# A spectral filter and an MLP on one core: the inverse column transform folded over f and -f, and sums moved between engines

## The chip, the core and the metric

The kernel runs on one core of a Trainium2 chip. A core has five engines that run at the same time, each with its own list of instructions: TensorE (PE in the profile; its weight loads are PEld) for matmuls and transposes, VectorE (DVE), ScalarE (ACT), GpSimd (POOL) and SyncE (SP), which here issues every DMA. Matmuls write into PSUM, eight banks of 128 partitions by 512 fp32 columns; all else lies in SBUF. An engine works through its list in order, and waits on semaphores for others. The metric is the device time of one execution in microseconds; lower is better. The median before is 391.79 us (three runs, 391.14 to 392.72).

## The reference

```python
mod = (_silu(c) @ w_mod).reshape(1, 6, 1, 512)
sa, ca, ga, sb, cb, gb = mod
h = layernorm(x) * (1 + ca) + sa                 # x: 2048 x 512
x = x + ga * irfft2(rfft2(h) * (w_r + 1j * w_i))
h = layernorm(x) * (1 + cb) + sb
x = x + gb * (mish(h @ w1 + b1) @ w2)            # w1: 512 x 1376, w2: 1376 x 512
```

Six vectors of 512, made from a conditioning vector c, shift, scale and gate two branches. The first branch is a filter in the frequency plane: a real two-dimensional FFT, a product with a complex weight, the inverse. The second is a dense layer, Mish, and a dense layer.

## The kernel before

There are no FFT instructions: the transforms are matmuls with constant matrices. The 2048 rows are split as 128 x 16, the 512 columns as 128 x 4, so that a transform is one matmul over 128 points and one small matrix over 16 and 4 points, which sits on the partitions (16 x 4 complex numbers are 128 real ones). One core does everything in four stages, and SBUF holds x throughout.

1. *Rows and columns forward* (0 to 50 us). For each n of 16, `p1_row` multiplies a transposed tile of x with row constants, and `p1_col` applies the column transform over 128 points. The result is `a_sb`.
2. *The frequency plane* (50 to 99 us, lines 374 to 597). The 64 column frequencies q go in 17 groups of up to four, in the order `seq`; group 0 (the frequencies 0, 64, 128 and so on) is special. For a group, `p2_in` transposes on TensorE and ScalarE copies to SBUF (GpSimd adds the shift's share to column 0), `p2_mul` multiplies with `kf` (the small transforms), `p2_prod` takes the complex product with the weights (two products on VectorE, a difference and a sum mostly on GpSimd), `p2_back` transposes back and ScalarE copies, `p2_out` multiplies with `kv` (the small inverse transforms), and `store_d` copies into `dd` on ScalarE, in three planes: real, imaginary, and minus real. The steps of different groups overlap in an order written out by hand (`manual_schedule`): step s does the products of group s, the `kf` matmuls of group s + 1, the copies in of group s + 3, the transposes back of group s - 2 and the `kv` matmuls of group s - 3. Between them stand pieces of the six vectors: `mod_fetch` loads a tile of `w_mod`, `mod_late` adds it up on VectorE (`mod_step` for the two gates, `mod_column` for scale and shift of the second norm), `mod_gate` multiplies the first gate into the row constants `kiv` (step 7), `apply_gate` spreads the second gate over all partitions by a matmul, at the stage's end.
3. *Columns and rows back* (99 to 146 us). `p3_col(n)` undoes the column transform with eight matmuls of 128 x 128: for each of four pieces, one over the planes real and imaginary with the constants `kc[0]` and one over imaginary and minus real with `kc[1]`. ScalarE copies the bank, `p3_row(n)` does four matmuls with `kiv`, and VectorE adds the result to x and takes the statistics of the second norm (`norm_sums`). Beside this, the MLP's weights are prepared: `load_w1` and `split_w1` cut w1 into a high and a low half (ScalarE casts, GpSimd subtracts), through two buffers; `load_w2`, `sum_w2` (GpSimd) and `split_w2` (ScalarE and VectorE) prepare w2 and sums of its blocks, which live in `modr[:, 0:2]`.
4. *The MLP* (146 to 389 us). Eight blocks of 256 rows, in each six pieces of the 1376 columns: `up`, `front`, `back` (Mish and four sums on VectorE, line 779), `halves` (high and low halves), `down`, where `down` runs two pieces behind `up`; `residual` multiplies with the second gate and adds to x.

SP's queue and each engine's list are in the order of the program. Buffers of the pool `work` come in twos per tag (`t`, `y`, `g1`, `g2`, `h`), and so do the PSUM banks A to D; a write waits for the last reader of the buffer before last. The tiles of the pool `big` share space by tag (`da`, `db`, `cr`, `ci`) from stage to stage.

## Time and profile before

| | |
|---|---|
| median of three runs | 391.79 us |
| the profiled execution | 391.52 us (span 389.4 us from the first to the last instruction) |
| TensorE busy | 383.1 us (98%) |
| VectorE, ScalarE, GpSimd busy | 298.8, 247.9, 96.1 us |
| bytes moved by DMA | 36.44 MB |
| granted TensorE clock | 1.000 |

In a line of a timeline stand the start in us, the duration, the engine, the line of the kernel, the operation, what is written and read, the shape, and the count where equal instructions are merged; in square brackets the idle time before and what ended it. A duration reaches from the start to the end on the engine, so it holds time in which the instruction was held up. One fp32 matmul stands as two instructions. In a table of stages each engine's busy time is given for the stretch named at the left, then the granted clock, the DMA engines' share and the rate.

### The profile page before, as it was taken

Reading aid. Unit: us, or ns where it says so; the run is one execution under the profiler, and the core shown is the slowest. Engines: PE = TensorE matmul, PEld = TensorE weight load, DVE = VectorE, ACT = ScalarE, POOL = GpSimd, SP = SyncE. Lnnn points to the kernel's source line nnn. Section 1 sums busy time; section 2 is a strip of 40 time slices with the busy share of each in tenths; the row PEclk is TensorE's granted clock in tenths of the full one; section 3 lists DMA queues with packets and bytes.
Section 4 is the critical chain, followed back from the end, with each engine's and each line's share of the span. In section 5 each row is a group of like instructions: output and inputs, shape, how many; then the busy total and the mean of one; then the engine's idle time right before and its main releaser. Section 6 shows DMA issues by size and latency. Waiting matters only on the chain.

```text
span 389.4 us, 7386 instructions
## 1 busy us (share of the span) xinstructions
PE 383.1 (98%) x2752; PEld 355.4 (91%) x2752; DVE 298.8 (77%) x668; ACT 247.9 (64%) x546; POOL 96.1 (25%) x132
## 2 busy tenths in 40 slices
PE   8999999999999999999999999999999999999996
PEld 8889889999999998999998998999999999899984
DVE  2888978876299989887856965965966875987993
ACT  1798756678559648975855765674674674594751
POOL 0687737665077533300000000000000010017000
PEclk9999999999999999999999999999999999999999
DMA  7999993472132411100100100100100200123011
GB/s 237 383 323 339 347 344 109 133 300 63 47 124 78 145 49 28 56 3 0 56 0 3 54 2 0 56 0 2 55 2 0 76 0 2 46 65 106 3 54 54
DMA packets 21027, 36.44 MB, mean 94 GB/s; under 512 B 3680, under 2 KB 6592, under 8 KB 20736
## 3 DMA queue, kind: packets, MB, share of 16 engines
q1 hardware_dynamic: 20992, 35.98, 27.1%
q8 instruction: 21, 0.34, 0.3%
q14 instruction: 14, 0.11, 0.1%
HBM read 31.78 MB, written 4.19 MB: 92 GB/s over the span
## 4 chain that ended last, share of the span: by engine, by line
PE 86%; DMA 4%; DVE 3%; ACT 3%; issue 1%; SPq 1%; POOL 1%; POOLq 0%; DVEq 0%
PE bank L805 24%; PE bank L752 20%; PE bank L754 10%; PE bank L482 3%; PE bank L528 3%; PE bank L673 3%; PE bank L663 3%; PE bank L664 3%; PE bank L797 2%; PE bank L248 2%; DMA x<-in_A_x_dram 2%; PE bank L203 2%; PE bank L817 2%; PE bank L642 2%; PE bank L461 2%; DMA mraw<-in_km_dram 2%
## 5 line engine op out<-in xcount | busy, mean ns | idle before, releaser
L762 ACT ACTIVATE buf<-bank,b1n 128x256 f32<-128x256 f32 (+1 forms) x88 | 40.8, 472 | 66.8 <-PE bank L754 66.4
L763 DVE TENSOR_TENSOR buf<-buf,bank 128x256 f32<-128x256 f32 (+1 forms) x88 | 35.4, 417 | 38.6 <-ACT buf L762 38.6
L715 DVE TENSOR_TENSOR al<-buf,ah 128x512 fp32r<-128x512 f32 (+2 forms) x85 | 53.5, 653 | 0.7 <-ACT ah L714 0.7
L734 POOL TENSOR_TENSOR buf<-buf,modr 128x512 f32<-128x512 f32 (+1 forms) x3 | 3.9, 1292 | 183.0 <-DMA buf<-in_B_w_dram 175.7
L752 PE MATMUL bank<-h2e,w1h 128*128 128x512 f32 (+1 forms) x176 | 48.4, 397 | 0.0
L752 PE MATMUL bank<-h2o,w1h 128*128 128x512 f32 (+1 forms) x176 | 48.3, 396 | 0.0
L714 ACT CAST ah<-buf 128x512 fp32r<-128x512 f32 (+2 forms) x85 | 43.0, 548 | 1.2 <-DVE buf L779 1.2
L779 DVE TENSOR_TENSOR buf<-buf 128x128 f32<-128x128 f32 x148 | 39.9, 311 | 3.5 <-ACT buf L769 2.2
L769 ACT ACTIVATE buf<-buf 128x512 f32<-128x512 f32 (+1 forms) x48 | 28.6, 596 | 14.8 <-DVE buf L763 14.7
L805 PE MATMUL bank<-w2a,ah 128*128 128x256 f32 x161 | 34.9, 286 | 0.0
L752 PEld LDWEIGHTS bank<-h2o,w1h 128*128 128x128 f32 (+1 forms) x176 | 30.2, 187 | 4.5
L752 PEld LDWEIGHTS bank<-h2e,w1h 128*128 128x128 f32 (+1 forms) x176 | 30.1, 187 | 4.5
L805 PE MATMUL bank<-w2b,ah 128*128 128x256 f32 x147 | 31.8, 283 | 0.0
L754 PEld LDWEIGHTS bank<-h2o,w1l 128*128 128x128 f32 (+1 forms) x176 | 26.7, 185 | 4.2
L754 PEld LDWEIGHTS bank<-h2e,w1l 128*128 128x128 f32 (+1 forms) x176 | 26.7, 185 | 4.2
L754 PE MATMUL bank<-h2e,w1l 128*128 128x256 f32 (+1 forms) x176 | 27.8, 280 | 0.0
L754 PE MATMUL bank<-h2o,w1l 128*128 128x256 f32 (+1 forms) x176 | 27.8, 280 | 0.0
L805 PEld LDWEIGHTS bank<-w2a,ah 128*128 128x128 f32 x161 | 26.7, 191 | 0.0
L663 PE MATMUL bank<-kc,d 128*128 128x128 f32 x128 | 24.7, 275 | 0.0
L664 PE MATMUL bank<-kc,d 128*128 128x128 f32 x128 | 24.7, 275 | 0.0
L805 PEld LDWEIGHTS bank<-w2b,ah 128*128 128x128 f32 x147 | 24.6, 191 | 0.0
L117 DVE BATCH_NORM_STATS2 st<-x 128x6 f32<-128x512 f32 x32 | 22.1, 689 | 0.8 <-DMA x<-in_A_x_dram 0.4
(227 smaller groups left out, 1002.7 us busy)
## 6 DMA issues: line engine op xcount, KB each, us to landing
buf<-in_B_w_dram SPq DMA_DIRECT2D x20, 256.0 KB, 2.8
x<-in_A_x_dram SPq DMA_DIRECT2D x16, 256.0 KB, 4.9
xring<-in_x_t_dram SPq DMA_DIRECT2D x16, 256.0 KB, 5.1
wm<-in_w_mod_dram SPq DMA_DIRECT2D x16, 256.0 KB, 4.2
out_dram<-x SPq DMA_DIRECT2D x7, 512.0 KB, 2.6
mraw<-in_km_dram SPq DMA_DIRECT2D x16, 128.0 KB, 5.0
wqa<-in_w_q_dram SPq DMA_DIRECT2D x8, 256.0 KB, 4.8
wqb<-in_w_q_dram SPq DMA_DIRECT2D x8, 256.0 KB, 5.5
```

Source lines behind the costliest of these rows:

```text
L117: nc.vector.bn_stats(t, x[:, n, :])
L663: nc.tensor.matmul(o, dj[:, 0:128], kc[0][:, n, :], start=True, stop=False)
L664: nc.tensor.matmul(o, dj[:, 64:192], kc[1][:, n, :], start=False, stop=True)
L714: nc.scalar.copy(h, r)
L715: nc.vector.tensor_tensor(l, r, plain(h), op=ALU.subtract)
L752: nc.tensor.matmul(ps, w1h[:, k, fs], h[:, k], start=(k == 0), stop=False)
L754: nc.tensor.matmul(ps[:, 0:256], w1l[:, k, fs], h[:, k, 0], start=False, stop=(k == 3))
L762: nc.scalar.activation(o, ps[:, 256:], AF.Identity, bias=b1n[:rows, f:f + 1])
L763: nc.vector.tensor_tensor(o, o, ps[:, 0:256], op=ALU.add)
L769: nc.scalar.activation(o, o, AF.Mish)
L779: nc.vector.tensor_tensor(o, p, q, op=op)
L805: nc.tensor.matmul(o, a[p][:, e], w2[t][q][:, r], start=(own and half == 0 and t == 1 and i == 0), stop=(end and i == 2 and (n, half) != ( ...
```

## The change

- `p3_col` has four matmuls of 128 x 128 instead of eight. For that, the frequencies f of the column transform are numbered so that partition p holds f = p for p under 64, f = -(p - 63) for 64 to 126, and 64 for partition 127 (constants and weights are laid out to match). On the way back, the sum and the difference of the values at f and -f are taken first (`fold`, VectorE: two instructions of 4 x 63 columns, one operand in SBUF and the other in the PSUM bank of the transpose). `dd` then has two planes and one set of constants `kc`; `store_d` has three copies, two of them on 63 partitions only.
- The fold of group s - 3 stands at step s, a step behind the copy, and `p2_out` moves from s - 3 to s - 4; there is a step more.
- The frequency 64 of every group is collected in `zh` by a small copy in `p2_in`, and goes through its own product and transforms (`half_mul`, `half_prod`, `half_back`, `half_out`) in steps 14 to 17; a DMA within SBUF puts it into partition 127 of `dd`.
- Group 0 is rewritten in the same manner: six copies and four folds instead of reversed copies.
- The first gate's sums run on GpSimd (`mod_step`: a scaling, and a sum for all but the first) in steps 3, 5, 7 and 9, and `mod_gate` in step 12. The second gate's sums run on GpSimd in the MLP, after its items 2 and 3, from one load of 1 MB behind the third stage; `apply_gate` runs after item 5.
- w1 goes through six buffers instead of two: two of `g2` and two each of the tags `ah` and `al`; five loads are issued at step 0 of the third stage.
- The low half of the sums of w2's tile 2 is computed on GpSimd, not VectorE. The places of some tiles in `big` change.

```diff
+H = P // 2
+U = P - 1
...
-    def mod_step(acc, w, k, eng):
-        one = sc[:, k:k + 1]
-        if k == 0:
-            eng.tensor_scalar(acc, w, one, 0.0, op0=ALU.mult, op1=ALU.add)
-        else:
-            eng.scalar_tensor_tensor(acc, w, one, acc, op0=ALU.mult, op1=ALU.add)
+    def mod_step(acc, w, k):
+        nc.gpsimd.tensor_scalar(w if k else acc, w, sc[:, k:k + 1], 0.0, op0=ALU.mult, op1=ALU.add)
+        if k:
+            nc.gpsimd.tensor_tensor(acc, acc, w, op=ALU.add)
...
-    def store_d(ps, q0, nq):
+    dd = big.tile([P, 4 * N2, 2, NQ], F32, name="dd", tag="dd")
+
+    def store_d(ps, q0, nq, end=U):
         src = ps[:, 0:nq * 128].rearrange("p (q a c) -> p a c q", q=nq, c=2)
-        for i in range(2):
-            dst = dd[i].rearrange("p n d c q -> p (n d) c q")
-            s = src[:, 32 * i:32 * i + 32]
-            nc.scalar.copy(dst[:, :, 0:2, q0:q0 + nq], s)
-            nc.scalar.mul(dst[:, :, 2, q0:q0 + nq], s[:, :, 0, :], -1.0)
+        qs = slice(q0, q0 + nq)
+        nc.scalar.copy(dd[0:H, :, :, qs], src[0:H])
+        nc.scalar.mul(dd[H:end, :, 0, qs], src[H:end, :, 1, :], -1.0)
+        nc.scalar.copy(dd[H:end, :, 1, qs], src[H:end, :, 0, :])
...
+    def fold(z, far):
+        nc.vector.tensor_tensor(z[..., H:U], z[..., 1:H], far, op=ALU.subtract)
+        nc.vector.tensor_tensor(z[..., 1:H], z[..., 1:H], far, op=ALU.add)
...
+    def half_out():
+        pd = bank("D")
+        nc.tensor.matmul(pd[:, 0:NQ], kv[:, 512:640], st.pop(("t", "h"))[:, 0:NQ], start=True, stop=True)
+        nc.scalar.copy(zh, pd[:, 0:NQ])
+        nc.sync.dma_start(dd[U:P].rearrange("p a c q -> p (a c) q")[:, :, 1:NQ], zh[:, 1:NQ])
...
-        t = buf("t")
-        nc.scalar.copy(t[:, 0:w], pc[:, 0:w])
-        st["t", g] = t
+        tv, src = (v[:, 0:w].rearrange("p (q s) -> p q s", s=P) for v in (buf("t"), pc))
+        nc.scalar.copy(tv[:, :, 0:H], src[:, :, 0:H])
+        st["t", g] = tv, src
...
-        for s in range(len(seq) + 3):
+        for s in range(len(seq) + 4):
             mod_fetch(s + 2)
+            if s >= 4:
+                p2_out(seq[s - 4])
+            if 3 <= s < len(seq) + 3:
+                p2_fold(seq[s - 3])
...
-            if s >= 3:
-                p2_out(seq[s - 3])
-            if s == 7:
+            if s == 12:
                 mod_gate()
...
+            for i, fn in enumerate((half_mul, half_prod, half_back, half_out)):
+                if s == len(seq) - 3 + i:
+                    fn()
...
-        r = buf("g2")[:, 0:hi - lo]
+        r = (buf("g2") if i % 3 == 0 else act.tile([P, 512], F32, name="wr", tag=("", "ah", "al")[i % 3]))[:, 0:hi - lo]
...
-        for j in range(4):
-            dj = d[:, j].rearrange("p c q -> p (c q)")
-            o = pe[:, j * P:(j + 1) * P]
-            nc.tensor.matmul(o, dj[:, 0:128], kc[0][:, n, :], start=True, stop=False)
-            nc.tensor.matmul(o, dj[:, 64:192], kc[1][:, n, :], start=False, stop=True)
+        for j in range(4):
+            nc.tensor.matmul(pe[:, j * P:(j + 1) * P], dd[:, 4 * n + j].rearrange("p c q -> p (c q)"), kc[:, n, :],
+                             start=True, stop=True)
...
-            split(h[:, 768:], l[:, 768:], tsum.rearrange("p e d -> p (e d)"))
+            split(h[:, 768:], l[:, 768:], tsum.rearrange("p e d -> p (e d)"), nc.gpsimd if t == 2 else nc.vector)
...
-        if s < 12:
-            load_w1(s)
+        for i in range(0 if s == 0 else s + 4, min(s + 5, 12)):
+            load_w1(i)
...
+    load_gate()
     split_w2(0, False)
...
         if s in (2, 3):
             split_w2(4, s == 3)
+            for k in (2 * s - 4, 2 * s - 3):
+                mod_step(modr[:, 2], late["g"][:, k], k)
+        if s == 5:
+            apply_gate()
```

160 lines of the change are left out of this document (99 added, 61 removed).

## The prediction, made before the changed kernel had run

> **What bounds the kernel now.** I read the page's busy shares first, then a table of stages, then the timelines of TensorE, VectorE and GpSimd around the third stage (columns back and rows back, lines 657 to 676) and on both sides of it, where the change works.
>
> ```profile
> span 389.4 us, 7386 instructions
> PE 383.1 (98%) x2752; PEld 355.4 (91%) x2752; DVE 298.8 (77%) x668; ACT 247.9 (64%) x546; POOL 96.1 (25%) x132
> ```
> ```profile
> core 0: us, PE busy (x) PEld busy (x) DVE busy (x) ACT busy (x) POOL busy (x), PEclk, DMA share, GB/s
> 50.20:98.90 48.70, 47.87 (x401) 45.24 (x401) 36.77 (x71) 33.81 (x104) 28.15 (x50) 1.00 0.53 186
> 98.90:146.30 47.40, 47.26 (x411) 46.55 (x410) 39.55 (x75) 27.96 (x57) 23.36 (x24) 1.00 0.27 83
> 150.20:173.00 22.80, 22.74 (x155) 20.72 (x156) 21.16 (x47) 19.41 (x39) 6.50 (x8) 1.00 0.08 26
> ```
>
> TensorE is busy everywhere, so each matmul taken away looks like a gain. But in the third stage VectorE is busy for 39.55 us too, and it idles until the first row sum at 103.58: between 103.58 and 146.3 it is nearly full.
>
> ```profile
> 102.49 1.06 PE L673 MATMUL bank<-kiv,buf 128*128 128x128 f32 x8
> 105.17 1.06 PE L673 MATMUL bank<-kiv,buf 128*128 128x128 f32 x8
> ```
> ```profile
> 103.58 0.69 DVE L676 TENSOR_TENSOR x<-x,bank 128x512 f32<-128x512 f32 x1 [8.42 <-PE bank L673]
> 106.26 0.69 DVE L676 TENSOR_TENSOR x<-x,bank 128x512 f32<-128x512 f32 x1 [1.05 <-PE bank L673]
> 110.05 1.14 DVE L130 SCALAR_TENSOR_TENSOR ve<-ve,rstd 128x2 f32<-128x2 f32 x1
> 115.70 0.16 DVE L130 SCALAR_TENSOR_TENSOR ve<-ve,rstd 128x2 f32<-128x2 f32 x1
> 116.09 1.26 DVE L142 SCALAR_TENSOR_TENSOR nmr<-mv,rstd 128x2 f32<-128x2 f32 x1
> 130.51 1.20 DVE L715 TENSOR_TENSOR w2a<-modr,w2a 128x1024 fp32r<-128x1024 f32 x1
> 140.73 0.65 DVE L676 TENSOR_TENSOR x<-x,bank 128x512 f32<-128x512 f32 x1
> 142.38 0.69 DVE L676 TENSOR_TENSOR x<-x,bank 128x512 f32<-128x512 f32 x1
> 144.66 0.69 DVE L676 TENSOR_TENSOR x<-x,bank 128x512 f32<-128x512 f32 x1 [0.64 <-PE bank L673]
> ```
> ```profile
> 109.90 1.27 POOL L622 TENSOR_TENSOR w1l<-buf,w1h 128x512 fp32r<-128x512 f32 x1
> 116.06 1.28 POOL L622 TENSOR_TENSOR w1l<-buf,w1h 128x512 fp32r<-128x512 f32 x1 [2.62 <-ACT w1h L621]
> ```
>
> A step of the stage is 105.17 - 102.49 = 2.68 us on TensorE: 12 matmuls (eight in the column step, four in the row step), 0.223 us each. VectorE needs about 1.5 us for a row where nothing else comes between (140.73 to 142.38 holds one row sum, its statistics and a 0.14 us gap), so 16 rows are 24 us; the weights' low halves, the input's low halves and the norms fill the rest. And it is held up: at 110.05 and 116.09 an instruction on two columns takes 1.14 and 1.26 us where the same kind takes 0.16 at 115.70, and each ends within 0.05 us of a GpSimd subtraction (109.90 + 1.27, 116.06 + 1.28). Over the stage I add up 7.5 us of such waits in eleven places (2.1 of them are these two), always in VectorE instructions with two operands in SBUF; the row sums, which read a PSUM bank, stay at 0.65 to 0.69.
>
> **The change, part by part.** Sums are against the profiled execution, 391.5 us (span 389.4), 0.3 us under the median of 391.79.
>
> *Third stage.* Four of twelve matmuls of a step go: 16 x 4 x 0.223 = 14.3 us of TensorE work, so a step needs 1.79. VectorE loses one instruction only, the 1.20 us at 130.51, which goes to GpSimd (at the 1.28 us for 512 columns above, some 2.5 for 1024). From the stage's start the first row sum comes after two column steps and a row step of four matmuls each: 3 x 0.89 = 2.7 us instead of 4.7, a gain of 1.9; with the 1.20 and the two idles (1.05 and 0.64, of which 0.3 stays) VectorE is through 4.5 us earlier. That is what bounds the stage afterwards; TensorE idles some 10 us in it. Against that, GpSimd has the same twelve subtractions and twelve sums and 2.5 us more, in a shorter stage: I raise the port waits by 1.3. Term B = -3.2. Its ends: -1 if the first norms (four instructions in a row, each behind a GpSimd one) cost 3.7 us as I walk them through; -10.7 if the 7.5 us of waits vanish.
>
> *Second stage (50 to 99).* Per group TensorE does what it did: 2.70 us.
>
> ```profile
> 77.23 1.06 PE L482 MATMUL bank<-kf,buf 128*128 128x128 f32 x8
> 79.93 1.06 PE L482 MATMUL bank<-kf,buf 128*128 128x128 f32 x8
> 82.64 1.06 PE L482 MATMUL bank<-kf,buf 128*128 128x128 f32 x8
> 97.06 1.16 PE L528 MATMUL bank<-kv,buf 128*128 128x128 f32 x8 [0.22 <-ACT buf L518]
> 98.05 1.02 PE L558 MATMUL bank<-modr,ones 128*128 128x512 f32 x2
> 70.97 1.02 PE L553 MATMUL bank<-modr,ones 128*128 128x512 f32 x2
> ```
> ```profile
> 87.53 1.28 DVE L498 TENSOR_TENSOR buf<-bank,wqb 128x512 f32<-128x512 f32 x2
> 73.83 0.68 DVE L110 SCALAR_TENSOR_TENSOR wm<-wm,modr 128x512 f32<-128x512 f32 x1
> 72.03 0.69 DVE L554 TENSOR_TENSOR kiv<-kiv,bank 128x512 f32<-128x512 f32 x1 [0.42 <-PE bank L553]
> 153.29 0.74 DVE L763 TENSOR_TENSOR buf<-buf,bank 128x256 f32<-128x256 f32 x2
> L100 DVE SCALAR_TENSOR_TENSOR modr<-wm,sc,modr 128x512 f32<-128x512 f32 x6 | 5.3, 882 | 0.0
> ```
>
> A fold is two instructions of 252 columns, one operand in PSUM, the second waiting for the first: by the pair at 153.29 (0.74) about 0.8. Sixteen add 12.5 us to VectorE; the sums that leave for GpSimd or the next stage take 6.5 away (5.3 for six, two smaller). 36.77 becomes about 43 of 48.7 us, and GpSimd's 28.15 about 35: while groups flow the slack of a step covers this, and I cost it at nothing; without that cover it is up to 0.4 us in each of 14 groups. ScalarE's copies stay equal in number of columns (half a copy less, wider storing copies, a copy of four columns). The split zero group costs six small copies for two and four sums for two, once; nothing while a step's slack holds.
>
> At the end of the stage nothing flows on. The gate's scaling (0.69) now comes in step 12, when its matmul is done: 82.64, less 0.87 for the gate that used to be at 70.97, plus matmuls and transposes of the step (1.8) and the gate (0.87), about 84.5. Behind it VectorE has in order 7 folds (5.6), four pairs of products (4 x 1.2), two column sums (1.4), two differences (0.8) and the 127th row's products (0.45): with the scaling 13.7 us, to 98.2. Then the last group's matmuls (0.89) and its three storing copies (about 1.05), which the matmul at 98.05 used to cover and no longer does: 100.1 against 98.9, +1.2. VectorE also waits for ScalarE, whose storing copies of an earlier group stand ahead of the last half copy, and TensorE for the row's sums on GpSimd; walked through, these make it +3.1. Term A = +2.2, between the two; +0.3 if VectorE is never late (the extra small matmuls).
>
> *Loads.* The second w1 load now waits for the last matmul with kv, and behind it on SP's queue stand three more and two of w2: at 0.43 us an issue and 2.8 to land (below) they are there 5 us after the stage's start, and VectorE comes to them after 6. The 3.0 us that ScalarE and GpSimd waited for w1 and the row that arrives by DMA (before ScalarE's last copies) cost nothing.
>
> ```profile
> 113.90 0.85 SPq L703 DMA_DIRECT2D buf<-in_B_w_dram  x2
> buf<-in_B_w_dram SPq DMA_DIRECT2D x20, 256.0 KB, 2.8
> ```
>
> *The second gate's sums* move behind the third stage: seven GpSimd instructions that wait for nothing once the four sums of w2's fifth tile are done (their load ends far earlier), while VectorE is 93% busy (21.16 of 22.80).
>
> ```profile
> 150.84 2.53 DVE L779 TENSOR_TENSOR buf<-buf 128x128 f32<-128x128 f32 x4
> 155.02 1.01 DVE L779 TENSOR_TENSOR buf<-buf 128x128 f32<-128x128 f32 x4
> 157.55 1.16 DVE L715 TENSOR_TENSOR al<-buf,ah 128x384 fp32r<-128x384 f32 x2
> ```
> ```profile
> 151.68 0.78 POOL L711 TENSOR_TENSOR modr<-buf 128x256 f32<-128x256 f32 x1
> L197 POOL TENSOR_SCALAR mring<-mring 128x256 fp32r<-128x256 f32 x16 | 6.8, 427 | 1.4
> ```
> ```profile
> 161.17 2.52 PE bank L805 x21
> ```
>
> Four subtractions on VectorE take 1.01 us alone and 2.53 beside three GpSimd sums of about 0.75: they take turns, one for one. Three additions at 1.28 and four scalings of 512 columns (0.427 for half of that; I take 0.75) are 6.8 us in a row, and put about 6.2 on VectorE. TensorE's slack there is 161.17 - (157.55 + 1.16) = 2.4. So 3.8 us of stall, and the gate's own 0.87 us matmul, now in this stage, lies mostly within it: term C = +4.0. Its ends: +0.9, if the scalings, with one SBUF operand, hold nobody and the additions fit the slack; +6.5. [...]
>
> Sum: 391.5 + 2.2 - 3.2 + 4.0 = 394.5.
>
> **The rivals.**
> 1. *Faster: the port waits of the third stage go.* TensorE runs ahead, ScalarE and GpSimd with it thanks to six w1 buffers, and GpSimd's subtractions fall where VectorE reads PSUM. Then B = -10.7: 387.0. For it: GpSimd waited 2.62 us for a cast at 116.06, so its place can move. Against: the same norms and low halves are still among the same GpSimd work. It beats the losses once the waits fall from 7.5 to about 4.
> 2. *No change: GpSimd's gate sums cost little,* C = +0.9: 391.4. For it: they may spread over gaps of VectorE; against: they wait for nothing and follow each other.
> 3. *VectorE late in every group,* 0.4 us in 14: +5.6, 400.1. Against: 43 of 48.7 us.
> 4. *TensorE's clock falls in the idle third stage.* The granted clock is 1.00 in every stretch above, with gaps that stay short; here 29 us of matmuls in 43. If it fell to half there, TensorE would need 58 us: about +14, 408. [...]
>
> **How the numbers follow.** Forecast 0.53 (its own range 392.5 to 397.5), rival 1 0.17, rival 2 0.20, rival 3 0.07, rival 4 0.03. 0.5% of 391.8 is 2 us, about what a measurement here tells from no change: 389.8 to 393.8. Faster is rival 1 and a little of rival 2, 0.20; same the rest of 2 and the forecast's lower edge, 0.22; slower 0.58. The range leaves out half of rival 1's spread and rivals 3 and 4: 387.3 to 398.5.
>
> **What would show it.** Right: third stage shorter by 2 to 5 us only, TensorE idle in it waiting for row sums, VectorE over 90%; its start at 100 to 102; VectorE's subtractions (L828 in the changed kernel) stretched behind GpSimd's scalings at about 150 to 160, and idle TensorE before the down products there. Wrong: row sums every 1.8 us; TensorE without gaps after 150; VectorE's tiny norm instructions at 0.16 us throughout.

## The result and the profile after

The changed kernel takes 409.16 us (median of four runs, 407.1 to 413.85); the kernel before took 391.96 beside it: 17 us slower, where the prediction had 3 us slower and a range up to 398.5. The profiled execution is the longest of the four (413.85 us, span 412.1) and counts as a slow run with a mean granted clock of 0.963, against 0.979 to 0.985 in the other three, whose median is 408.5: the ratio of 1.042 (95% interval 1.037 to 1.047) and every gain or loss named below go by these three. So the profile shows more falls of the clock than a usual run has; experiment 2 measures the stages with a steady clock.

First the page of the changed kernel: span, busy times, and the granted clock in 40 slices.

```profile
span 412.1 us, 7207 instructions
PE 385.7 (94%) x2629; PEld 356.3 (86%) x2629; DVE 312.4 (76%) x694; ACT 250.3 (61%) x553; POOL 112.5 (27%) x151
PEclk9999999699979779989999999999999999999999
```

TensorE has 64 column matmuls less and is busy for longer than before, 385.7 against 383.1 us. The third line says why: the granted clock, 9 in every slice before, is lower in several, down to 6. The table of stages shows where the span went; the columns are those of the prediction's table. The stages are cut at the same instructions in both kernels: the zero group's first transpose, the first column matmul of the third stage, the first `down` matmul, the end. Before:

```profile
52.91:98.92 46.01, 45.31 (x381) 42.90 (x380) 34.57 (x67) 32.22 (x101) 27.55 (x47) 1.00 0.50 174
98.92:150.16 51.24, 51.09 (x433) 49.78 (x431) 42.91 (x84) 31.68 (x66) 23.63 (x25) 1.00 0.27 82
150.16:389.40 239.24, 235.59 (x1582) 215.67 (x1581) 181.23 (x411) 148.22 (x301) 16.21 (x15) 1.00 0.08 28
```

After:

```profile
53.15:112.76 59.61, 49.58 (x383) 46.64 (x382) 42.94 (x94) 35.11 (x106) 33.79 (x57) 0.94 0.25 86
112.76:167.45 54.69, 46.35 (x304) 44.51 (x304) 43.91 (x83) 30.51 (x63) 25.57 (x26) 0.82 0.36 108
167.45:412.10 244.65, 238.25 (x1584) 217.46 (x1583) 185.55 (x411) 148.81 (x302) 24.36 (x22) 0.99 0.08 28
```

The second stage is 13.6 us longer, the third 3.45 us longer although a third of its matmuls is gone, the MLP 5.4 us longer: 22.5 us in this one execution, where the usual run is 16.5 us longer. Inside each lies a wait or a chain of waits. In the second stage GpSimd has the first gate's scaling and sum (L100, L102) and then a group's difference and sum ahead of the zero group's two memsets (L441, L442), and ScalarE, VectorE and TensorE wait for these one behind the other. It is the queue that holds the memsets, not their buffers: GpSimd has no gap from 66.05 us on, and the second buffer's last readers, matmuls with `kv` that begin at 68.24, end at 69.3.

```profile
67.59 0.69 POOL L100 TENSOR_SCALAR wm<-wm,sc 128x512 f32<-128x512 f32 x1
68.37 1.27 POOL L102 TENSOR_TENSOR modr<-modr,wm 128x512 f32<-128x512 f32 x1
71.55 0.41 POOL L441 MEMSET buf<- 128x384 f32 x1
71.90 0.20 POOL L442 MEMSET buf<- 96x128 f32 x1
72.00 0.21 ACT L443 COPY buf<-bank 128x64 f32<-128x64 f32 x1 [3.13 <-POOL buf L441]
72.93 0.69 DVE L456 TENSOR_TENSOR buf<-buf,bank 128x63 f32<-128x63 f32 x4 [2.73 <-POOL buf L442]
73.20 0.94 PE L462 MATMUL bank<-kv,buf 128*128 128x128 f32 x6 [2.11 <-DVE buf L456]
```

At the end of the stage TensorE runs with gaps. From the second last group's first products (95.40) to the third stage (112.76) are 17.36 us; before, the same way was 88.04 to 98.92, 10.88 us.

```profile
95.40 1.06 PE L524 MATMUL bank<-kf,buf 128*128 128x128 f32 x8
97.46 0.40 PE L469 MATMUL bank<-kf,zh 128*64 128x128 f32 x2 [0.53 <-ACT buf L560]
100.04 1.13 PE L524 MATMUL bank<-kf,buf 128*128 128x128 f32 x8 [1.10 <-DVE buf L540]
...
103.79 0.27 PE L485 MATMUL bank<-ident,buf 64*128 64x64 f32 x1 [0.78 <-ACT dd L384]
...
110.32 1.12 PE L576 MATMUL bank<-kv,buf 128*127 128x128 f32 x8 [1.34 <-DVE buf L397]
112.76 3.79 PE L714 MATMUL bank<-kc,dd 128*128 128x128 f32 x16 [1.32 <-ACT dd L384]
```

Before, the last groups' matmuls with `kv` followed each other like this:

```profile
94.41 1.06 PE L528 MATMUL bank<-kv,buf 128*128 128x128 f32 x8
95.78 1.06 PE L528 MATMUL bank<-kv,buf 128*128 128x128 f32 x8
```

In the third stage the 1024-column subtraction that went to GpSimd holds an instruction of VectorE on four columns for as long as it runs, 2.28 us (0.16 in experiment 10, where the subtraction is back on VectorE):

```profile
144.23 2.35 POOL L764 TENSOR_TENSOR w2a<-modr,w2a 128x1024 fp32r<-128x1024 f32 x1
144.33 2.28 DVE L132 SCALAR_TENSOR_TENSOR ve<-ve,rstd 128x4 f32<-128x4 f32 x1
```

At the MLP's start VectorE's four subtractions stretch beside the second gate's scalings and sums, as the prediction had it. ScalarE waits for them, and behind ScalarE TensorE, at the next block's transposes:

```profile
172.35 1.61 POOL L102 TENSOR_TENSOR modr<-modr,gate 128x512 f32<-128x512 f32 x1
172.72 3.58 DVE L828 TENSOR_TENSOR buf<-buf 128x128 f32<-128x128 f32 x4
176.34 0.63 ACT L763 CAST ah<-buf 128x512 fp32r<-128x512 f32 x1 [2.40 <-DVE buf L828]
179.75 0.33 PE L696 MATMUL bank<-ident,buf 128*128 128x128 f32 x1 [2.17 <-ACT buf L155]
```

The second of the four by itself, beside a scaling alone (173.94 to 174.67); without GpSimd beside it one takes 0.28 us:

```profile
174.14 0.66 DVE L828 TENSOR_TENSOR buf<-buf 128x128 f32<-128x128 f32 x1
```

And behind waits of this kind comes something that the prediction held for unlikely: the granted clock falls. Here are stretches of 3.41 us of the changed kernel, laid so that one begins where the clock first falls; the first busy time is TensorE's, the third number from the right is the granted clock:

```profile
70.89:74.30 3.41, 1.30 (x10) 0.98 (x9) 1.33 (x6) 2.22 (x10) 1.21 (x4) 1.00 0.43 144
74.30:77.71 3.41, 2.69 (x13) 2.66 (x13) 3.24 (x7) 1.39 (x6) 2.54 (x5) 0.51 0.00 0
77.71:81.13 3.42, 3.42 (x18) 3.42 (x17) 1.92 (x6) 1.57 (x4) 2.80 (x4) 0.50 0.29 96
81.13:84.54 3.41, 3.41 (x32) 3.41 (x31) 1.47 (x4) 2.48 (x9) 1.74 (x4) 0.99 0.91 366
...
108.43:111.84 3.41, 1.67 (x13) 1.32 (x12) 0.83 (x2) 2.29 (x7) 0.00 (x0) 1.00 0.00 0
...
125.50:128.91 3.41, 1.76 (x16) 1.60 (x16) 3.27 (x7) 0.00 (x0) 2.06 (x3) 1.00 0.37 90
128.91:132.32 3.41, 1.34 (x13) 1.15 (x11) 3.25 (x9) 3.22 (x6) 1.27 (x1) 1.00 0.61 199
...
145.97:149.39 3.42, 0.48 (x5) 0.29 (x3) 3.32 (x5) 1.68 (x4) 3.41 (x4) 1.00 0.00 0
...
176.69:180.10 3.41, 1.22 (x7) 0.75 (x5) 3.38 (x7) 2.02 (x4) 2.02 (x2) 1.00 0.59 142
```

The clock fell to 0.50 at 74.4, 111.9, 132.4, 149.5 and 180.2 us, five times, and each time the stretch before it is one in which TensorE was busy for 0.48 to 1.67 of 3.41 us. After 125.50:128.91, with 1.76, it did not fall. It came back to 0.99 after stretches with 3.42 us of work (77.71:81.13) and, at 183.5, with 3.07. At 0.50 a step of four matmuls takes 1.71 us (78.63 to 80.34) instead of 0.89.

### The profile page after: what moved, and what is told of

The parts are those of the page before. It is cut to its first block, busy times and chain, and to the rows that moved or that the text cites. A ratio compares the mean times of both kernels' runs of the same rounds, so it can differ in the third digit from the quotient of the medians.

```text
span 412.1 us, 7207 instructions
## 1 busy us (share of the span) xinstructions
PE 385.7 (94%) x2629; PEld 356.3 (86%) x2629; DVE 312.4 (76%) x694; ACT 250.3 (61%) x553; POOL 112.5 (27%) x151
## 4 chain that ended last, share of the span: by engine, by line
PE 73%; DVE 12%; ACT 4%; DMA 4%; issue 3%; POOL 3%; SPq 1%; POOLq 0%; DVEq 0%; ACTq 0%
PE bank L854 22%; PE bank L801 18%; PE bank L803 9%; PE bank L724 3%; DVE buf L540 3%; PE bank L714 3%; DMA x<-in_A_x_dram 2%; PE bank L251 2%; PE bank L206 2%; PE bank L846 2%; PE bank L866 2%; PE bank L524 2%; PE bank L696 2%; PE bank L576 2%; DMA mraw<-in_km_dram 1%
## 5 line engine op out<-in xcount | busy, mean ns | idle before, releaser
L828 DVE TENSOR_TENSOR buf<-buf 128x128 f32<-128x128 f32 x148 | 43.5, 335 | 3.5 <-ACT buf L818 2.2
L854 PE MATMUL bank<-w2c,ah 128*128 128x256 f32 x196 | 35.8, 283 | 0.0
L854 PEld LDWEIGHTS bank<-w2c,ah 128*128 128x128 f32 x196 | 30.4, 191 | 0.0
L724 PE MATMUL bank<-kiv,buf 128*128 128x128 f32 x128 | 21.7, 324 | 8.3 <-DVE x L727 5.4
L854 PE MATMUL bank<-w2c,al 128*128 128x256 f32 x98 | 27.7, 283 | 0.0
L724 PEld LDWEIGHTS bank<-kiv,buf 128*128 128x128 f32 x128 | 19.7, 235 | 9.0 <-issue 5.8
L714 PE MATMUL bank<-kc,dd 128*128 128x128 f32 x128 | 21.0, 320 | 1.3 <-ACT dd L384 1.3
```

The source lines that it names most:

```text
L714: nc.tensor.matmul(pe[:, j * P:(j + 1) * P], dd[:, 4 * n + j].rearrange("p c q -> p (c q)"), kc[:, n, :], start=True, stop=True)
L724: nc.tensor.matmul(px[:, j * P:(j + 1) * P], e[:, j * P:(j + 1) * P], kiv[:, j, :], start=True, stop=True)
L828: nc.vector.tensor_tensor(o, p, q, op=op)
L854: nc.tensor.matmul(o, a[p][:, e], w2[t][q][:, r], start=(own and half == 0 and t == 1 and i == 0), stop=(end and i == 2 and (n, half) != ( ...
```

## The experiments

Two theories stood at the start. *Queues:* what an engine has standing ahead of a short instruction (memsets, small steps, sums) makes the others wait, and the clock falls in time that was lost anyway. *Clock:* the waits are short, and the falls that they set off cost most. Stage lengths below are of the profiled executions, one each; times are medians, and gains are against 408.5 us.

**1. Which engine bounds the third stage.** The kernel before, with half of the column step left out.

```diff
-            nc.tensor.matmul(o, dj[:, 0:128], kc[0][:, n, :], start=True, stop=False)
-            nc.tensor.matmul(o, dj[:, 64:192], kc[1][:, n, :], start=False, stop=True)
+            nc.tensor.matmul(o, dj[:, 0:128], kc[0][:, n, :], start=True, stop=True)
```

> The kernel before, with the second matmul of each column pair in the third stage left out (64 matmuls of 0.223 us, 14.3 us of TensorE work; so a part of the backward column transform is not computed). Nothing else is moved. If TensorE's work bounds that stage: 391.8 - 14.3 = 377.5 us. If VectorE bounds it, as the prediction says, the stage loses the 1.9 us of its start and the two idles: 388 to 390 us. If the granted clock falls when TensorE has gaps in that stage, some of the stage's matmuls take 1.7 us a row step instead of 0.89 and the time is 391 or more, with a granted clock of 0.5 in a stretch of 7 us inside the third stage.

388.44 us against 391.41, ratio 0.992 (0.990 to 0.994). The table of stages, third stage:

```profile
98.43:146.68 48.25, 39.96 (x306) 37.48 (x304) 42.11 (x84) 31.27 (x66) 23.87 (x25) 0.96 0.29 87
```

14.3 us of TensorE work are worth 3.0 us. VectorE, busy for 42.11 of the 48.25 us, bounds the stage behind its first row sum, and a fall of the clock in it (mean 0.96) did no visible harm, I think because TensorE (39.96) was not the late one.

**2. The clock alone.** Matmuls that nobody reads fill the gaps of the changed kernel.

```diff
+    def fill(ps, count):
+        for _ in range(count):
+            nc.tensor.matmul(ps[:, 0:P], ones, ones, start=True, stop=True)
...
         pe = bank("A")
+        fill(pe, 6 if n == 0 else 0)
+        if 4 <= n < 15:
+            fill(bank("C"), 4)
```

> The changed kernel plus matmuls that nobody reads (ones times ones, 128 columns, into a bank that is overwritten right behind), put where TensorE waits: before the zero group's last matmuls, in the last groups of the second stage, in steps 0 and 4 to 14 of the third, and before two transposes of the MLP. It is work added, nothing is taken away. Theory of the clock: the waits themselves stay, but the granted clock stays at 1.00, and the 6 to 8 us that the clock's falls take go: 399 to 403 us against 408. Theory of the queues: TensorE only waits with its hands full, the clock's falls are hidden behind the same waits: 408 to 411.

406.23 us (405.89 to 406.42), with a granted clock of 1.00 throughout:

```profile
52.63:111.24 58.61, 53.18 (x443) 50.46 (x441) 42.71 (x94) 35.16 (x106) 33.61 (x57) 1.00 0.28 95
111.24:160.86 49.62, 47.14 (x392) 45.58 (x393) 44.45 (x83) 30.60 (x63) 25.86 (x26) 1.00 0.38 119
160.86:404.50 243.64, 238.88 (x1599) 217.90 (x1599) 185.16 (x411) 148.90 (x302) 24.28 (x22) 1.00 0.08 28
```

Work added made it 2.3 us faster, less than the theory of the clock had. But the fillers cost something themselves: 1.55 us at the second stage's end (18.91 instead of 17.36 us behind the second last group's first products), and 0.85 in the third stage by one profiled execution each (experiment 12). Without these it would be 403.8 by my estimate, and the falls would cost 4.7 us. The four runs of the changed kernel give a little more: their mean clocks, 0.963 to 0.985, stand for 15.2 to 6.1 us of missing clock (the span times what the mean lacks to 1), and their spans, 412.1 to 405.3, differ by 0.75 us for each of these; at 0.979, the clock of two of the four, that is 8.5 x 0.75 = 6.4 us. So the falls cost some 5 to 6 of the 17 us. Neither theory alone is right; the larger part is the queues'.

**3. The zero group's memsets.** Its two buffers in a tile of their own, cleared at the stage's start.

```diff
-        t1, t2 = buf("t"), buf("t")
-        nc.gpsimd.memset(t1[:, 0:3 * P], 0.0)
-        nc.gpsimd.memset(t2[0:96, 0:P], 0.0)
+        t1, t2 = zt[:, 0:384], zt[:, 384:512]
...
     with tc.manual_schedule():
+        nc.gpsimd.memset(zt, 0.0)
```

> The changed kernel with the zero group's two operand buffers in a tile of their own, cleared once at the start of the second stage, so that no memset stands on GpSimd's queue behind the scalings and sums, and no wait for those buffers. Theory of the queues: the 3.1 to 3.4 us stall at 70 to 75 us goes, 404 to 406 us against 408. Theory of the clock: with that gap the clock's first fall goes too (74.4 to 81.1 at half, 3.4 us of work lost): 400 to 402.

404.8 us, 3.7 less. TensorE's wait ahead of the zero group's last matmuls is gone, and the clock's first fall with it:

```profile
71.83 0.83 PE L460 MATMUL bank<-kv,zt 128*128 128x128 f32 x6
```

From the group before (70.02) to the next (73.19) are 3.17 us, in the changed kernel 69.12 to 75.08, 5.96.

**4. The second gate's sums on GpSimd.** Six of their seven instructions left out.

```diff
-            for k in (2 * s - 4, 2 * s - 3):
-                mod_step(modr[:, 2], late["g"][:, k], k)
+            if s == 2:
+                mod_step(modr[:, 2], late["g"][:, 0], 0)
```

> The changed kernel with only the first of the seven GpSimd instructions of the second gate's sums (the rest of that gate's columns is left out, so the gate is not the whole one). If these sums take turns with VectorE's subtractions, as the prediction says, the MLP's start loses 4 to 5 us: 403 to 405 against 408, and the subtractions beside them take 1.0 us for four instead of 3.6. With the clock's fall at 180 gone too: one to two more. If they cost nothing because TensorE waits for something else: 408.

405.36 us, 3.1 less; from the first `down` matmul to the end:

```profile
161.51:401.70 240.19, 236.39 (x1584) 215.98 (x1583) 181.56 (x411) 148.80 (x302) 16.98 (x16) 1.00 0.08 28
```

240.19 us against 244.65 with the sums (in an execution whose clock also falls at 180.2) and 239.24 before. The four subtractions that took 3.58 us beside them take 1.01 and 1.02 where no sum runs. Here the prediction named the right cause.

**5. The second gate's sums on VectorE.** As in the kernel before, but meant for VectorE's idle time at the third stage's start.

```diff
+    def gate_sums():
+        acc, one = modr[:, 2], late["g"]
+        nc.vector.tensor_scalar(acc, one[:, 0], sc[:, 0:1], 0.0, op0=ALU.mult, op1=ALU.add)
+        for k in range(1, 4):
+            nc.vector.scalar_tensor_tensor(acc, one[:, k], sc[:, k:k + 1], acc, op0=ALU.mult, op1=ALU.add)
...
             p3_col(s)
+        if s == 0:
+            gate_sums()
```

> The changed kernel with the second gate's sums as four instructions on VectorE (about 0.69 us each) at the third stage's start, where VectorE waits 7 us for the first row sum, from a buffer that is loaded in the second stage, and the gate's matmul in step 4 of the third stage. Nothing is left out. If GpSimd's sums cost the MLP's start 4 to 5 us by taking turns with VectorE: 403 to 405 us, as with all but one of them left out, and from the first down product to the end 240 us. If a loss comes back in the third stage (VectorE later at the first row sum): 407.

406.08 us, 2.4 less. The MLP is as short as before (the last row below), but the four sums did not stay where they were written: that code is outside the order written by hand, and they ran at 89.9 to 98.6, among VectorE's products of the last groups. In the profiled execution, again the longest of its four (409.88), the second stage took 64.76 us instead of 59.61, just what the MLP gave back; the clock, 0.89 there instead of 0.94, has a part in that.

```profile
53.34:118.10 64.76, 52.48 (x383) 49.02 (x381) 45.77 (x98) 35.20 (x106) 34.86 (x57) 0.89 0.30 102
...
168.60:408.10 239.50, 235.66 (x1581) 215.61 (x1581) 181.59 (x411) 148.12 (x301) 16.24 (x15) 1.00 0.08 28
```

**6. The end of the second stage: VectorE's column sums, the fold's step, the order.** Three ways to shorten it that all missed. First the last four column sums moved behind the last products:

```diff
-    for i, s in enumerate((3, 5, 7, 9, 4, 6, 8, 10, 11, 12, 13, 14)):
+    for i, s in enumerate((3, 5, 7, 9, 4, 6, 8, 10, 17, 18, 19, 20)):
```

> The changed kernel with the last four column sums of w_mod (VectorE, about 0.76 us each) taken out of steps 11 to 14 and put into steps 17 to 20, where VectorE waits for ScalarE's half copies. Theory that VectorE is full in the last groups (folds 0.84, products 1.28 and a column sum 0.76 or more to a step of 2.70 us, and the gate's scaling): the third stage begins 3 us earlier than the 12.7 us behind the last group's first products allow now, 405 to 406 us against 408. Theory that the way behind the last products sets the stage's end (mul, products, sums, copy, fold, out, stores, each behind the other): it stays at 408, since the sums come back there.

407.15 us. From the last group's first products to the third stage it stayed at 12.7 us (98.39 to 111.12; 100.04 to 112.76 in the changed kernel). Second, the last three groups folded right behind their half copy:

```diff
-            if 3 <= s < len(seq) + 3:
+            if 3 <= s <= 16:
                 p2_fold(seq[s - 3])
...
                 p2_back(seq[s - 2])
+                if s >= 16:
+                    p2_fold(seq[s - 2])
```

> The changed kernel with the last three groups folded in the step of their half copy instead of one step later, and their matmuls with kv one step earlier (20 steps instead of 21). If the additional step behind the last products is what costs: from the last group's first products to the third stage's first matmul 12.7 us become 10 to 11, 406 to 407 us against 408. If VectorE's being late in the groups before it costs: no change, 408.

412.95 us, 4.4 us slower. Now copy, fold, matmuls and stores of one group stand behind each other before the next group's transposes may begin: the last three groups' matmuls with `kv` begin at 103.91, 108.35 and 113.10 us, 4.4 and 4.75 apart instead of some 2.4. The clock is at 0.50 there for 17 us, which is a part of it (eight matmul instructions take 2.05 us at 108.35 and 113.10 instead of 1.06); in experiment 7, with the same edit and a mean clock of 0.987 instead of 0.971, they are still 3.83 apart. The step that the change puts between copy and fold is worth its place. Third, transposes and half copies ahead of the multiplications and of the stores:

```diff
+            if s >= 15:
+                if s < 20:
+                    p2_fold(seq[s - 3])
+                if s < 17:
+                    p2_prod(seq[s])
+                if s < 19:
+                    p2_back(seq[s - 2])
+                if s < 16:
+                    p2_mul(seq[s + 1])
+                p2_out(seq[s - 4])
```

> The changed kernel with another order in the last steps of the second stage (from step 15 on): the transposes and the half copy of group s-2 stand ahead of the multiplications of the next group and of the matmuls with kv and their three storing copies of group s-4, on TensorE's and ScalarE's queues; one more buffer for the half copies makes that possible. Theory that the end of the second stage is a ring of three queues in order (TensorE's matmuls with kv, ScalarE's three storing copies ahead of the next half copy, VectorE's fold, TensorE again): the 12.7 us from the last group's first products to the third stage become 9 to 10, 404 to 406 us against 408. Theory that only VectorE's own work is too much there: no change, 408.

409.66 us, no gain: TensorE now waits 1.8 us for ScalarE's copy of the 127th row, which stands behind the stores. The wait has moved, not gone.

**7. Four repairs together:** experiments 3 and 5 and the first two edits of 6.

> All four repairs together: the zero group's buffers of their own, the last column sums behind the last products, the last three folds at once, the second gate's sums on VectorE at the third stage's start. The second stage should end at 101 to 104 us instead of 112.8, the MLP start with its old pace. By the theory of the queues alone (the single gains 4.4 + 3 + 2 + 4.5): 395. With the clock's falls gone as well where the gaps went: 390 to 393, no slower than the kernel before. If the gaps only move: 400.

403.93 us, 4.6 less. The single gains do not add up: with the zero group mended, the end of the second stage took longer than ever (20.58 us from the second last group's first products, 89.84 to 110.42, instead of 17.36), with the folds at once and the gate's sums in it.

**8. The 127th row.** What was left at the stage's end were its four small steps, which take one of two banks and buffers each. Left out, with only the row's DMA kept:

```diff
-            for i, fn in enumerate((half_mul, half_prod, half_back, half_out)):
-                if s == len(seq) - 3 + i:
-                    fn()
+            if s == len(seq) - 1:
+                nc.sync.dma_start(dd[U:P].rearrange("p a c q -> p (a c) q")[:, :, 1:NQ], zh[:, 1:NQ])
```

> The changed kernel with the four steps of the 127th row left out (its product with kf, the products with the weights, the transpose, the matmul back; the row that is sent to dd by DMA is then not the right one). Theory that this row costs the end of the stage by taking one of two banks and buffers from the last groups: from the second last group's first products to the third stage 17.4 us become 13 to 14, 404 to 405 us against 408. Theory that the folds' additional step is what costs: 17, and 407 to 408.

404.95 us, 3.6 less. From the second last group's first products to the third stage are 14.73 us instead of 17.36, and the last group's now begin 2.26 us behind them instead of 4.64:

```profile
92.55 1.06 PE L524 MATMUL bank<-kf,buf 128*128 128x128 f32 x8
94.81 1.06 PE L524 MATMUL bank<-kf,buf 128*128 128x128 f32 x8
...
107.28 2.05 PE L713 MATMUL bank<-kc,dd 128*128 128x128 f32 x16 [1.32 <-ACT dd L384]
```

Moved two steps later instead (`len(seq) - 1 + i`):

> The changed kernel with the 127th row's four steps two steps later, behind the last group's first products; nothing is left out. By the theory of the banks: most of what leaving the row out gains, 404 to 406 us, less what the row's DMA then adds at the stage's end (it lands 2 us after its issue). By the theory of the folds' step: 408, or later by that DMA.

406.7 us: about half of it. The last group's first products again begin 2.26 us behind the others (93.09 and 95.35), but the third stage then waits 2.05 us for the row's DMA, which in the changed kernel lands 2.9 us after its issue, where 2 were expected.

```profile
108.95 3.75 PE L714 MATMUL bank<-kc,dd 128*128 128x128 f32 x16 [2.05 <-DMA dd<-zh]
```

**9. Do the row and the column sums hide each other?** Both edits in one kernel.

> The changed kernel with the four steps of the 127th row left out (as in the run that left out that row alone) and the last four column sums in steps 17 to 20. If the two hide each other's gain: from the second last group's first products to the third stage 11 to 12.5 us (17.4 in the changed kernel, 14.7 without the row, 17.0 with the columns moved), 402 us or less. If the folds' additional step costs the rest by itself: 14 to 14.7, 404 to 405.

405.44 us.

```profile
95.21 1.06 PE L524 MATMUL bank<-kf,buf 128*128 128x128 f32 x8
...
109.54 3.68 PE L713 MATMUL bank<-kc,dd 128*128 128x128 f32 x16 [1.32 <-ACT dd L384]
```

14.33 us, the second of the two expectations. So the 6.5 us of the stage's end are 2.6 for the row, 0.4 for the column sums, and about 3.5 that neither explains. I put these down to the fold's place in the chain (half copy behind the stores of another group, fold, matmuls, stores, none beside other work). In this run's timeline TensorE waits 0.39 and 1.32 us for folds and 0.91 and 1.32 us for storing copies behind 95.21; before, it waited 0.22 us there, and the second gate's matmul (0.87) stood in front of the third stage. That it is the rest is shown, its cause only read from the timeline.

**10. The 1024-column subtraction back on VectorE**, with the fillers of experiment 2.

```diff
-            split(h[:, 768:], l[:, 768:], tsum.rearrange("p e d -> p (e d)"), nc.gpsimd if t == 2 else nc.vector)
+            split(h[:, 768:], l[:, 768:], tsum.rearrange("p e d -> p (e d)"), nc.vector)
```

> The kernel with the matmuls that nobody reads (so with a granted clock of 1.00 everywhere), and the 1024-column subtraction of w2 given back to VectorE from GpSimd. If the 2.35 us instruction on GpSimd holds VectorE's norms as long as it runs, so that the move gains nothing: the third stage goes from 49.6 us to 48.3 to 49 and the time from 406.2 to about 405. If the move is worth the 1.2 us that VectorE would need for it: 407.4.

406.18 us against 406.23, no difference in the time; in one profiled execution each the third stage is 48.76 us long instead of 49.62. The instruction that took 2.28 us takes 0.16 again:

```profile
139.35 0.16 DVE L132 SCALAR_TENSOR_TENSOR ve<-ve,rstd 128x4 f32<-128x4 f32 x1
```

So the move of 1.2 us to GpSimd gained nothing; that it cost 0.9 us, as the stage has it, the times do not show.

**11. The w1 buffers alone**, in the kernel before.

```diff
-        r = buf("g2")[:, 0:hi - lo]
+        r = (buf("g2") if i % 3 == 0 else act.tile([P, 512], F32, name="wr", tag=("", "ah", "al")[i % 3]))[:, 0:hi - lo]
...
-        if s < 12:
-            load_w1(s)
+        for i in range(0 if s == 0 else s + 4, min(s + 5, 12)):
+            load_w1(i)
```

> The kernel before with the six w1 buffers and the earlier w1 loads of the change, nothing else. The prediction costs them at nothing: 391.4 to 391.8 us. If the early loads hold something on SP's queue or in the buffers of the MLP: 393 or more; if ScalarE's casts had been waiting for w1 to some effect: 390 or less.

391.69 us against 391.67, ratio 1.000 (0.998 to 1.002): nothing, as predicted.

**12. The repairs together.** Three versions, each with the zero group's buffers, the gate's sums on VectorE in the hand-written order at the second stage's end, the subtraction on VectorE and four fillers a step in the third stage. The first has the order of experiment 6's third edit, the second the row two steps later, the third the row's steps in 15, 16 and 18 and the column sums late.

> Several repairs in one kernel: the zero group's own buffers, the last steps' order as in the run beside it, the second gate's sums on VectorE in steps 17 to 20 of the second stage and its matmul in the third, the 1024-column subtraction on VectorE, and four unread matmuls a step in the third stage to keep the clock. Theory of queues and clock together: second stage 4 to 6 us longer than before, third stage 2.5 shorter, the MLP as before (240 us from the first down product): 392 to 395. If the gaps move somewhere else: 399 or more.

> Zero group's own buffers and its first memset at the stage's start, the 127th row two steps later, the second gate's sums on VectorE in steps 17 to 20 and its matmul in the third stage, the 1024-column subtraction on VectorE, four unread matmuls a step in the third stage. By the theories so far (397.9 of the version before it, less 3 to 4 for the row, less 1 for the memset, less 1 for the clock's fall there): 392 to 394. If the end of the stage stays as it is: 397.

> The repairs together, everything computed: the zero group's own buffers and first memset ahead, the 127th row's matmul with kf in step 15, its products in step 16, its transpose and matmul back in step 18, the last column sums in steps 17 to 20, the second gate's sums on VectorE behind the last fold and its matmul in the third stage, the 1024-column subtraction on VectorE, four unread matmuls a step in the third stage. Against 397.6 for the version before it: the row's DMA is no longer late (2.1) and VectorE is in time at the last products (2): 393 to 394. If the end of the stage does not move: 396 or more.

397.91, 397.63 and 395.4 us. The third, stage by stage:

```profile
53.88:105.17 51.29, 45.78 (x383) 43.56 (x382) 44.46 (x97) 35.00 (x106) 31.71 (x54) 1.00 0.32 111
105.17:155.28 50.11, 47.87 (x395) 45.96 (x395) 45.60 (x85) 31.23 (x65) 23.75 (x25) 1.00 0.33 98
155.28:394.70 239.42, 235.58 (x1581) 215.66 (x1581) 181.32 (x411) 148.33 (x301) 16.23 (x15) 1.00 0.08 28
```

The MLP has its old length (239.24), the third stage is 1.1 us shorter than before, and the second still 5.3 us longer (46.01), most of it at its end. The time is 1.0 per cent above that of the kernel before (0.8 to 1.2). Last, the same version without the fillers:

> The version of the run of 395.4 us without its four unread matmuls a step in the third stage. If the clock's falls in the third stage only fill time in which TensorE would wait anyway: 395.4. If they make TensorE the late one: granted clock at 0.50 in two or three stretches of 7 us there, the third stage 51 to 55 us instead of 50.1, 397 to 399.

394.89 us, ratio to the kernel before 1.009 (1.004 to 1.013), not to be told from 395.4. In the profiled execution the third stage is 49.26 us long, 0.85 shorter than with the fillers, though the clock fell once in it:

```profile
133.89:137.30 3.41, 1.19 (x11) 1.22 (x11) 3.34 (x6) 0.94 (x2) 2.17 (x4) 1.00 0.00 0
137.30:140.71 3.41, 3.41 (x19) 3.41 (x18) 3.34 (x6) 0.59 (x1) 2.46 (x3) 0.51 0.07 17
```

VectorE is busy for 3.34 us of both stretches: here, as in experiment 1, where VectorE was the late engine, the fall cost nothing that can be seen. In the changed kernel two of the falls began where TensorE is the late engine: behind the zero group (74.4 to 81.2 us), and ahead of the first row sum (111.9 to 118.7). What each of the five cost is not measured. No version found is faster than the kernel before.

## Why the prediction was right in direction and wrong in size

The prediction's sum by its own steps. The measured column is from the profiled execution of experiment 2, so at a clock of 1.00, less the 1.55 us of its fillers at the second stage's end:

| step | predicted | measured |
|---|---|---|
| second stage, lead (first groups) | 0 | +0.9 |
| second stage, zero group | 0 | +3.0 |
| second stage, groups that flow | 0 | +0.7 |
| second stage, its end (A) | +2.2 | +6.5 |
| third stage (B) | -3.2 | -1.6 (-2.5 without its fillers' 0.85) |
| MLP (C) | +4.0 | +4.4 |
| the clock's falls | 0 | +5 to 6 |

(The parts of the second stage: to the group before the zero group 15.98 us against 15.08; from there to the next group 5.98 against 3.84, of which 0.87 was the gate's matmul that moved on; 17.74 against 16.21 to the second last group, less the same 0.87; 17.36 against 10.88 from there. The rows add up to 18 us and more with -2.5 for the third stage, a little over the 16.5 to 17 of the times; each rests on one execution.)

**What bounds the kernel: right.** The prediction refused to count 14.3 us of matmuls as a gain, since VectorE is nearly full behind the first row sum; experiment 1 gives 3.0 us for them.

**C, right in cause, its number in part by luck.** The subtractions were held up beside GpSimd (3.58 us instead of 1.01). That its scalings hold them too, which the +4.0 counts in, no run had shown when the prediction was made; the changed kernel shows it once, in the subtraction beside a scaling alone (0.66 us instead of 0.28). The MLP lost 4.4 us with a steady clock (and eight fillers in its wait), and 4.5 us come back without the sums. But two parts of the working were too large and the total hid it: VectorE's stretched instructions lost 3.8 us (2.6 in the subtractions, 1.2 in three pairs of low halves), not 6.2, and TensorE waited 2.55 us (2.17 and 0.38), not 3.8, at the next block's transposes behind ScalarE instead of before the `down` products. What fills the rest of the 5.4 us of the profiled execution is the gate's own matmul (0.87) and the clock's fall at 180.2. The loads of w1, costed at nothing, cost nothing (experiment 11).

**B, right in mechanism, half to three quarters of the size.** The step mis-sized is "I raise the port waits by 1.3". That a port makes these waits no run shows; what the runs show is VectorE's instructions held up beside GpSimd's. The 1024-column subtraction on GpSimd, estimated at some 2.5 us and measured at 2.35, fell on a chain of VectorE's norm instructions and held one for 2.28 us; given back, the stage was 0.9 us shorter in one execution (experiment 10).

**A, the step that failed.** The prediction had +2.2 us for the whole second stage; it measured +11.1. Three terms in it were wrong. First, "The split zero group costs six small copies for two and four sums for two, once; nothing while a step's slack holds": it cost 3.0 us, and the price was not the copies but two memsets, 0.4 and 0.2 us long, that stand on GpSimd's queue behind the first gate's scaling (0.69) and sum (1.27), which the same change had put there. TensorE stood for 2.1 us and then for 0.7. The prediction names no memset; nor did it the one of the zero group's first tile, behind which TensorE waits 0.9 us in the lead. Second, of the row that goes by itself only 0.45 us of products and a DMA were counted; it cost 2.6 us. Without it, or with it two steps later, the last group's first products follow 2.26 us behind the ones before instead of 4.64, which fits four small steps that take turns in two banks with the last groups. Third, for the stage's end VectorE's instructions were added up to 98.2 and a chain of 1.9 us was put behind, +1.2; the waits between the engines were walked through to +3.1, and the prediction took the middle. What is left of the end without the row and the column sums is 3.5, so the walk was near the truth and the adding up was not: every later step passes TensorE, ScalarE, VectorE and TensorE again with nothing beside it, 2.4 us a step (110.32 to 112.76) where before it was 1.37 (94.41 to 95.78). "While groups flow the slack of a step covers this" was nearly right: 0.7 us over six groups, where rival 3 had 0.4 for each.

**The clock, rival 4, given 0.03.** It came, not where it was put (14 us from an idle third stage) but behind single waits in all three stages, 5 to 6 us in all; that its 408 lies near the measured time is chance. That the clock can fall, and to half, no run had shown when the prediction was made: it is 1.00 in every stretch of the kernel before. In the changed kernel it fell to 0.50 five times, 37.6, 20.5, 17.1 and 30.7 us apart, which is 11, 6, 5 and 9 times 3.41, and no idle stretch of that length stands ahead of a fall: TensorE was busy for 0.48 to 1.67 of the 3.41 us before each. The first came behind the zero group's wait of 2.1 us, in a place that the prediction put at nothing. Rivals 1 and 2 did not come: VectorE's waits for GpSimd stayed in the third stage, and the gate's sums cost 4.4, not 0.9.

The direction was given a chance of 0.58, and the range ended at 398.5, since A's own ends were +0.3 and +3.1 and the clock had almost nothing. Of the signs named for "right", the stretched subtractions came; the third stage, shorter by 2 to 5 us there, was 1.6 to 2.5 us shorter at a steady clock, and its start, at 100 to 102 there, was at 112.76. So the direction was right, as the signs of A, B and C were, but most of the loss lies in terms that the prediction put at nothing or next to it.

## What to carry to other kernels

A short instruction cost here what stood ahead of it on its queue: TensorE waited 2.11 us behind two memsets of 0.41 and 0.20 us. When a change adds work to an engine's list, look for every memset, small copy and half-size group on that list and for who waits for it. At the end of a stage, where nothing flows on, walk one step through all engines in order; adding up the busiest engine's work gave too little here, +1.2 where the end without the row and the column sums measured +3.5. And a wait of TensorE was not over when it ended: behind each of five stretches of 3.41 us in which TensorE was busy for 0.48 to 1.67 us, the granted clock stood at 0.50 for 3.4 or 6.8 us, 5 to 6 of the 17 us by the estimate of experiment 2. So read the granted clock behind each such wait.

## What the runs showed that was not expected

- The granted clock fell after stretches of 3.41 us in which TensorE was busy for about half or less: in the changed kernel 0.48, 1.22, 1.30, 1.34 and 1.67 us were followed by a fall and 1.76 was not; in experiment 12's last version 1.19 was and 1.69 was not. Busy time as the profile has it does not part the two: in experiment 6's second edit a stretch with 1.83 us (100.8 to 104.2) was followed by a fall. In the changed kernel the clock stayed at 0.50 for one stretch (3.4 us, at 180.2) or two (6.8, at 74.4) and came back after one in which TensorE was busy for 3.07 us or more; after 2.5 to 2.74 us it stayed low. In experiment 6's second edit it stayed low for 17 us, five stretches.
- Matmuls that nobody reads made the changed kernel faster: 164 more instructions on TensorE (2793 against 2629), 2.3 us less. Put where VectorE was the late engine they gave nothing (395.4 us with them, 394.89 without, experiment 12).
- A GpSimd instruction on 1024 columns held a VectorE instruction on four columns for 2.28 us, which by itself takes 0.16. Experiment 10 shows both.
- VectorE's four gate sums ran ahead of where they were written, at 89.9 to 98.6 us, and the second stage grew by 5.2 us in the profiled execution (experiment 5). In the hand-written order behind the last fold (the third version of experiment 12) they ran at 103.1 to 105.2 us, ahead of the first row sum, where VectorE has nothing else to do.
